# Attention products in two column groups of 64 output rows, run in groups

## The chip, the cores and the metric

The kernel runs on one core of a Trainium2 chip. Its engines work side by side and wait for each other through semaphores: TensorE (PE; PEld is its weight load) multiplies, VectorE (DVE), ScalarE (ACT) and GpSimd (POOL) do the elementwise work, and SyncE (SP) issues most of the transfers. The metric is the device time in microseconds of one execution; a profile of one execution shows what each engine did when.

TensorE multiplies a stationary operand of up to 128 x 128, which is loaded first, by a moving operand. The loaded operand's columns become the rows of the output. In the profile `128*128 128x64` is a product with 128 rows and 128 columns of weights, whose output has 64 elements in each row. A product of plain f32 operands shows as two records, a transpose or a product of the feed-forward's fp32r operands as one.

## What is computed

First a gated linear attention over 4 batches, 8 heads, 768 steps and 48 channels a head; then, on its output `x` (4 x 768 x 384), a Fourier transform over sequence and channels, and a normalized feed-forward layer with 1536 hidden channels:

```python
state = np.zeros((B, H, D, D), dtype=np.float32)
for t in range(S):
    state = alpha[:, :, t, :, None] * state + np.einsum('bhd,bhe->bhde', k[:, :, t], v[:, :, t])
    y[:, :, t] = np.einsum('bhd,bhde->bhe', q[:, :, t], state)
...
u = x + np.real(np.fft.fft(np.fft.fft(x, axis=1), axis=2))
un = (u - mu) / np.sqrt(var + 1e-06)
ch = np.maximum(un @ w_ch1, 0.0) @ w_ch2
return u + ch
```

## The kernel before

The attention takes two heads at a time: a pair lies in 112 partitions, one head in 0 to 47, the other in 64 to 111. The sequence is cut into six chunks of 128 steps. For each of the 16 pairs the function `attn_stages` has eight stages:

- s1 to s3 (DVE mostly): running products of alpha within the chunks, keys divided and queries multiplied by them (`R` and `A`), and the factors `mt` by which the state decays from chunk to chunk.
- s4: five TensorE transposes of the keys to `kt` (128 steps x 112), copied out by ACT.
- s5: the scores of each chunk, one product for each head. Head 0 has its 48 weight rows in partitions 0 to 47, head 1 in 64 to 111, so the two stand in different row groups of the array. ACT copies the scores to `X`, POOL's `affine_select` cuts them to the causal half.
- s6: for each of five chunks one product of keys and values, 112 x 96, both heads at once (line 865). Half of each result mixes the keys of one head with the values of the other; ACT builds masked decay factors `mh` (two operations, line 868), and the DVE multiplication of line 869, which brings the result from PSUM to `tt`, clears that half. Four DVE updates (line 874) then add each chunk's state to the decayed one of the chunk before.
- s7: for each of six chunks, scores times values, one product for each head with 128 output rows and 64 columns (line 888), and, from the second chunk on, queries times state, both heads at once, 96 columns (line 894). Three chunks share a PSUM tile `py`, which ACT copies to the batch's `y` tiles.
- s8: sums and differences for the Fourier transform (DVE).

`mix_stages` then does the transforms with TensorE products and DVE additions, `norm_stages` the normalization with transposes, and `ffn_stages` the feed-forward in 432 products a batch of 384 moving columns each.

Nothing is issued in the order in which it is written. Each call becomes an `Op` in a `Plan`, which simulates all engines with durations of its own (`duration`) and places the instructions one by one (`simulate`): for each engine the operation that is ready first, and among those ready at once the one with the smallest key. The key of batch b's feed-forward is b*1000 + 500 and it is marked `fill`; that of the next batch's attention is b*1000 + 420. So on TensorE attention goes ahead whenever it is ready, and feed-forward fills the rest. The first batch's attention has nothing to fill it and keys below 0; there the planner puts products of a tile of zeros (`zero`, lines 1331 and 1333) into TensorE's long gaps. PSUM is eight banks: three `a`, two `f1`, three `f2`; attention of later batches has the three `a` alone.

Every instruction passes through line 552, so the profile tells them apart by tiles: `a<-vn,w` (also `vn,x`, `wt,x`) is scores times values, `a<-tt,w` queries times state, `a<-vn,kt` keys times values, `a<-w,al` the scores, `a<-cst,al` the transposes of s4, `f<-x,wt` and `f<-wt,h` the feed-forward.

Of the kernel before, what the change touches and what calls it, by code (L numbers as in the profile page):

```python
# [16 lines left out]
AF = mybir.ActivationFunctionType  # L17
ALU = mybir.AluOpType
AX = mybir.AxisListType

B, H, S, D = 4, 8, 768, 48
DM = H * D
DFF = 4 * DM
P = 128
NT = S // P
# [7 lines left out]
CW = 112  # L33
GRP = 64
# [34 lines left out]
LONG = 3.0  # L69
FIRST = 2.8  # L70
NEAR = 3.0
LATE = 4.0
FAR = 12.0
SHORT = 20.0
# [120 lines left out]
class Plan:  # L195
# [120 lines left out]
    def duration(self, op, named, engine):  # L316
        n = op.free
        if "dma" in op.name:
            return 1.05 if engine == "POOL" else 0.05
        if engine == "PE":  # L320
            m = self.region(named["1"])[4]
            if op.name == "transpose":
                return max(m, self.region(named["2"])[4]) / 1200 + 0.002
            if str(named["1"].real(self.base(named["1"])).dtype).endswith("float32"):
                slow = 1.65 if self.stride(named["2"]) > 16 else 1.0
                p0, p1 = self.region(named["1"])[0:2]
                return max(m, slow * n) / (1100 if p1 - p0 <= GRP else 600) + 0.004
            return n / 2240 + 0.003
        if engine == "ACT":
            pointer = 0.094 if any(isinstance(named.get(k), View) for k in ("bias", "scale")) else 0.0  # L330
            slow = 1.8 if self.stride(named["out"]) > 16 and n > 64 else 1.0
            return (0.11 if self.psum(named.get("1")) else 0.14) + slow * n / 1200 + pointer + (0.25 if "accum_out" in named else 0.0)
        if op.name == "memset":
            return n / (960 if engine == "DVE" else 1100) + 0.01
        if engine == "DVE":
            if op.name == "bn_stats":
                return 0.47
            if op.name == "reciprocal":
                return 0.07 + n / 160
            if op.name == "tensor_tensor_scan":  # L340
                return 0.1 + n / 480
            if isinstance(named.get("scalar1"), View):
                return 0.09 + n / 1200
            whole = "bitcast" in [s[0] for s in named.get("out", View(None)).steps]
            pointer = 0.06 if isinstance(named.get("scalar"), View) else 0.0
            return 0.09 + pointer + n / (1920 if whole and op.name == "tensor_scalar" else 960)
        return 0.126 + n / 1094 if op.name == "affine_select" else 0.15 + n / 477
# [44 lines left out]
    def simulate(self, ghost=False, guess=None):  # L392
        ops = self.ops
# [35 lines left out]
        def finish(op, e):  # L429
            t = max(clock[e], start(op, e))  # L430
            return (max(t, held[other[e]]) if op.port and e in held else t) + op.durs[e]
# [4 lines left out]
            due = coming[e][0][0] + shift if coming[e] else 1e9  # L436
            return t + op.durs[e] > due + HOLD[e] and t < due + GRACE

        placed = 0
        while placed < len(ops):  # L440
            placed += 1
            best, spare = None, None
            for e, cand in wait.items():
                if not cand:
                    continue
                now = clock[e]
                times = []
                for n in cand:
                    op = ops[n]
                    t = start(op, e)  # L450
                    if t is None:
                        continue
                    if len(op.engines) > 1:
                        if any(finish(op, o) < finish(op, e) - SLACK[e] for o in op.engines if o != e):
                            continue
                    times.append((t, max(now, t), n))
                if not times:
                    continue
                free = [x for x in times if not blocks(ops[x[2]], e, x[1])] if guess else times
                for some, held_back in ((free, False), (times, True)):  # L460
                    if not some or (held_back and free):
                        continue
                    first = min(x[1] for x in some)
                    key, n, t = min((ops[n].key, n, max(t, now)) for t, late, n in some if late <= first + WINDOW[e])
                    if held_back:
                        if spare is None or t < spare[0]:
                            spare = (t, n, e)
                    elif best is None or t < best[0]:
                        best = (t, n, e)
            best = best or spare  # L470
            assert best is not None, "no instruction can be placed"
            t, n, engine = best
            op = ops[n]
            done[n] = True
            for e in op.engines:
                wait[e].remove(n)
            op.engine, op.dur = engine, op.durs[engine]
            if guess and op.crit:
                for x in coming.values():
                    while x and done[x[0][1]]:  # L480
                        x.pop(0)
                shift = t - guess[n][0]
# [22 lines left out]
            if "dma" in op.name:  # L505
                if op.loose:
                    end = t + (NEAR if op.key < 0 else FAR)
                else:
# [61 lines left out]
def gla_mix_ffn(ctx: ExitStack, tc: tile.TileContext, alpha, chunked, kq, pairkq, v, w1, w2, consts, rowtab, out):  # L570
    nc = tc.nc
    plan = Plan({"PE": nc.tensor, "ACT": nc.scalar, "DVE": nc.vector, "POOL": nc.gpsimd, "SP": nc.sync})
    V, A, G, T, SY = (Engine(plan, e) for e in ("DVE", "ACT", "POOL", "PE", "SP"))
# [45 lines left out]
    def fixed(shape, name, dtype=F32):  # L619
        return plan.fixed(cp.tile(shape, dtype, name=name))  # L620
# [4 lines left out]
    wts = [None] * (NW // 2)  # L625
    loaded = {}
    tts = [fixed([P, NT - 1, 2, D], f"tt{i}") for i in range(2)]
    mhs = [fixed([P, NT - 1, 2], f"mh{i}") for i in range(2)]
    d1 = fixed([P, S], "d1")
    back = fixed([P, S], "back")  # L630
    rec = fixed([P, NC], "rec")
# [2 lines left out]
    ceps = fixed([P, 1], "ceps")  # L634
    zero = fixed([P, 32], "zero")
    ones = fixed([P, 1], "ones")
    hm = fixed([P, 2], "hm")
    rows = fixed([P, 3], "rows", I32)
    bs = fixed([P, 1], "bs")
    fl = fixed([1, 1], "fl", I32)  # L640
# [44 lines left out]

    def setup():
        V.memset(zero, 0.0)
        for hd in range(2):
            V.memset(hm[:, hd : hd + 1], 0.0)
            for r0, n in ((0, 32), (32, 16)):  # L690
                V.memset(hm[GRP * hd + r0 : GRP * hd + r0 + n, hd : hd + 1], 1.0)
        V.memset(d1, 0.0)
        V.memset(back, 0.0)
        V.memset(back[:, C - 1 :: 2 * C], 1.0)
        V.memset(cm63, -63.0)
        V.memset(ceps, 1e-6)
        V.memset(ones, 1.0)
        V.memset(bad, 0.0)
        A.activation(zero[:, 0:1], zero[:, 0:1], AF.Square)
# [44 lines left out]
    def attn_stages(b, hp, i, mixed, last):  # L744
        tt = tts[i]
        pair, tid = b * NP2 + hp, b * NT3 + hp
        first = tid == 0
        e = last if hp == NT3 else {}
# [113 lines left out]
        def s6():  # L862
            pu = psa()
            for a in range(NT - 1):
                T.matmul(pu[0:CW, a * 2 * D : (a + 1) * 2 * D], e["kt"][:, a], loaded["vn", pair][:, 2 * a * D : 2 * (a + 1) * D], start=True, stop=True)
            mh, mt = mhs[i], e["mt"]
            for hd in range(2):
                A.activation(mh[0:CW, :, hd], mt[0:CW, 0 : NT - 1], AF.Copy, scale=hm[0:CW, hd : hd + 1])
            V.tensor_tensor(
                out=tt[0:CW], in0=pu[0:CW, 0 : (NT - 1) * 2 * D].rearrange("p (a h e) -> p a h e", h=2, e=D),  # L870
                in1=mh[0:CW, :, :, None].broadcast_to([CW, NT - 1, 2, D]), op=ALU.mult,
            )
            for a in range(1, NT - 1):
                V.scalar_tensor_tensor(
                    out=tt[0:CW, a], in0=tt[0:CW, a - 1], scalar=mt[0:CW, a : a + 1], in1=tt[0:CW, a], op0=ALU.mult, op1=ALU.add,
                )

        def s7():
            X = e["X"]
            ytiles = mixed()[0]  # L880
            for h2 in range(2):
                py = psa()
                for c in range(3):
                    cc = 3 * h2 + c
                    cs = slice(cc * P, (cc + 1) * P)
                    o = c * 2 * GRP
                    for hd in range(2):
                        T.matmul(
                            py[:, o + hd * GRP : o + (hd + 1) * GRP], X[h2][:, hd, c], loaded["vn", pair][:, (2 * cc + hd) * D : (2 * cc + hd) * D + GRP],
                            start=hd == 0, stop=cc == 0 and hd == 1,  # L890
                        )
                    if cc:
                        yo = py[:, o : o + 2 * GRP].rearrange("p (h e) -> p h e", h=2)[:, :, 0:D]
                        T.matmul(yo, e["A"][0:CW, cs], tt[0:CW, cc - 1], start=False, stop=True)
                yo = py[:, 0 : 6 * GRP].rearrange("p (a h e) -> p a h e", a=3, h=2)[:, :, :, 0:D]
                FL["ev"].copy(ytiles[h2][:, :, hp * 2 * D : (hp + 1) * 2 * D].rearrange("p a (h e) -> p a h e", h=2), yo)

# [389 lines left out]
    for i, f in enumerate(mixing()):  # L1287
# [3 lines left out]
        n = MIX[i] if i < len(MIX) else 0  # L1291
# [214 lines left out]
```

## Time and profile before

| | us |
|---|---|
| median of 3 runs | 504.91 (504.34 to 505.05) |
| the profiled execution | 504.47 |
| its span, first to last instruction | 502.8 |

The profile lists records: start, length, engine, what is written from what, and the shape. Records on PE overlap, since a product's record lasts from its start to the last of its results; the pace of a stream is the distance between starts. A row `start, us, ... xN` of the timeline is N records of one kind in sequence, its length up to the end of the last. A row of the groups gives busy time, mean length in ns, and the idle time of the engine before them with what ended it. A row of the windows gives for each engine the busy time and number of records in a stretch (PE, PEld, DVE, ACT and POOL in this order), then granted clock and transfers.

Where the batches stand in the trace: the first batch's attention runs to 49 us and its transforms to about 70 us; feed-forward of batch 0 starts at 70.2 us and its last product at 189.5, with the second batch's attention (91 to 144 us) and transforms between; that of batch 1 runs from 189.8 to 305.0 with the third's, that of batch 2 from 305.1 to 420.3 with the last one's; feed-forward of batch 3 runs alone from 420.4 us to the end.

### The profile page before, as it was taken

The numbers are of one execution on the slowest core, as the hardware profiler recorded it, in microseconds if no ns is written. First come the engines' busy times: TensorE is split into PE (matmuls) and PEld (weight loads), VectorE is DVE, ScalarE is ACT, GpSimd is POOL, SyncE is SP. The second block draws the span as 40 slices with busy tenths as digits, with TensorE's granted clock in tenths as the row PEclk, the third lists the DMA queues.
The fourth block names the chain that finished last, engine by engine and source line by source line (L and its number), as shares of the span: only waits on it lengthen the run. The fifth ranks groups of instructions, "written<-read, shape, count | busy, mean of one in ns | idle before, by whom it ended". The sixth has DMA issues, their size and how long they took to land.

```text
span 502.8 us, 9312 instructions
## 1 busy us (share of the span) xinstructions
PE 492.5 (98%) x3740; PEld 474.2 (94%) x3740; DVE 312.5 (62%) x685; ACT 187.6 (37%) x413; POOL 65.8 (13%) x83
## 2 busy tenths in 40 slices
PE   7999999999999999999999999999999999999995
PEld 6899989999999999999999999999999999999994
DVE  8877989897779997546799216736585114113112
ACT  4487386537752254532223115323222113111110
POOL 0421222203212001212200001212300000000000
PEclk9999999999999999999999999999999999999998
DMA  8869323337432113521303001200201001001001
GB/s 298 298 192 355 125 64 102 104 73 261 158 104 96 24 56 97 149 107 44 108 1 125 17 0 48 50 25 2 95 0 50 0 1 47 1 1 47 1 0 53
DMA packets 17681, 42.47 MB, mean 84 GB/s; under 512 B 2688, under 2 KB 8000, under 8 KB 17632
## 3 DMA queue, kind: packets, MB, share of 16 engines
q1 hardware_dynamic: 16576, 39.39, 23.5%
q0 software_dynamic: 768, 2.36, 1.7%
q8 instruction: 31, 0.51, 0.4%
q14 instruction: 18, 0.15, 0.1%
q10 hardware_dynamic: 288, 0.07, 0.1%
HBM read 31.97 MB, written 7.08 MB: 78 GB/s over the span
## 4 chain that ended last, share of the span: by engine, by line
PE 95%; ACT 1%; DMA 1%; POOL 1%; SPq 0%; DVE 0%; issue 0%; ACTq 0%
PE f L552 65%; PE a L552 27%; PE f L1333 1%; DMA al<-in_chunked_dram 1%; PE f L1331 1%; PE a L1331 1%; POOL x L552 1%; SPq L552 0%; ACT c L552 0%; DVE y L552 0%; ACT x L552 0%; ACT h L231 0%; ACT L552 0%; ACT f L552 0%; ACT kt L552 0%
## 5 line engine op out<-in xcount | busy, mean ns | idle before, releaser
L552 PE MATMUL f<-wt,h 128*128 128x384 f32 x864 | 178.9, 344 | 0.4 <-ACT h L231 0.4
L552 PE MATMUL f<-x,wt 128*128 128x384 f32 x864 | 176.5, 342 | 0.0
L552 PEld LDWEIGHTS f<-wt,h 128*128 128x128 f32 x864 | 150.3, 188 | 2.3 <-ACT h L231 0.8
L552 PEld LDWEIGHTS f<-x,wt 128*128 128x128 f32 x864 | 150.4, 188 | 1.2 <-issue 0.2
L552 DVE SCALAR_TENSOR_TENSOR h<-f,h 128x384 fp32r<-128x384 f32 x96 | 53.1, 554 | 123.6 <-ACT h L231 122.8
L231 ACT ACTIVATE h<-f 128x384 fp32r<-128x384 f32 x96 | 47.0, 491 | 185.0 <-PE f L552 179.6
L552 POOL TENSOR_SCALAR_AFFINE_SELECT w<-w 128x384 f32<-128x384 f32 x48 | 33.1, 711 | 199.9 <-ACT w L552 199.9
L552 PE MATMUL a<-vn,w 128*128 128x64 f32 x288 | 41.3, 265 | 0.0
L552 PEld LDWEIGHTS a<-vn,w 128*128 128x128 f32 x288 | 39.5, 191 | 0.0
L552 ACT COPY w<-a 128x384 f32<-128x384 f32 (+4 forms) x59 | 26.2, 482 | 26.2 <-PE a L552 26.1
L552 PE MATMUL a<-tt,w 112*128 112x96 f32 x144 | 28.0, 282 | 0.0
L552 DVE TENSOR_TENSOR y<-y,a 128x192 f32<-128x192 f32 (+4 forms) x66 | 20.5, 361 | 8.6 <-PE a L552 8.4
L552 PEld LDWEIGHTS a<-w,al 48*128 48x128 f32 x306 | 19.8, 187 | 5.8 <-ACT w L552 2.2
L552 PE MATMUL a<-w,al 48*128 48x128 f32 x306 | 24.9, 289 | 0.0
L552 ACT COPY y<-a 128x288 f32<-128x288 f32 x29 | 11.6, 399 | 31.9 <-PE a L552 31.8
L552 PEld LDWEIGHTS a<-tt,w 112*128 112x128 f32 x144 | 22.3, 191 | 0.5
L552 DVE TENSOR_TENSOR_SCAN w<-al,d 128x768 f32<-128x768 f32 (+1 forms) x13 | 21.1, 1624 | 2.1 <-PE a L552 1.1
L552 DVE SCALAR_TENSOR_TENSOR y<-f,r,y 128x384 f32<-128x384 f32 x30 | 17.3, 613 | 8.0 <-PE f L552 7.9
L552 DVE SCALAR_TENSOR_TENSOR tt<-tt,w 112x96 f32<-112x96 f32 x64 | 21.2, 331 | 1.3
L552 DVE TENSOR_TENSOR tt<-a,mh 112x480 f32<-112x480 f32 x15 | 9.8, 654 | 19.0 <-PE a L552 19.0
L552 DVE TENSOR_TENSOR_SCAN al<-al,back 128x768 f32<-128x768 f32 (+1 forms) x13 | 21.2, 1633 | 0.2 <-DVE w L552 0.2
L552 POOL DMA_INDIRECT y<-scr,rows x12 | 14.8, 1237 | 48.2 <-DMA scr<-y 45.7
(130 smaller groups left out, 557.3 us busy)
## 6 DMA issues: line engine op xcount, KB each, us to landing
kq<-in_kq_dram SPq DMA_DIRECT2D x10, 768.0 KB, 7.0
wt<-in_w_dram SPq DMA_DIRECT2D x8, 768.0 KB, 7.0
out_dram<-y SPq DMA_DIRECT2D x24, 192.0 KB, 1.9
al<-in_chunked_dram SPq DMA_DIRECT2D x11, 392.0 KB, 3.8
vn<-in_v_dram SPq DMA_DIRECT2D x14, 296.0 KB, 3.1
wt<-in_w_dram SPq DMA_DIRECT2D x8, 384.0 KB, 3.8
scr<-y SPq DMA_DIRECT2D x4, 576.0 KB, 3.7
w<-w SPq DMA_DIRECT2D x28, 48.3 KB, 2.1
```

What stands on the lines that cost most here:

```text
L231: return lambda out, x: e.activation(out, x, AF.Relu)
L552: op.ins = op.fns[op.engine](*[real(a) for a in op.args], **{k: real(x) for k, x in op.kwargs.items()})
L1331: short = lambda *b: nc.tensor.matmul(bank(*b)[0:32, 480:512], zero.real(), zero.real(), start=True, stop=True)
L1333: long = lambda *b: nc.tensor.matmul(bank(*b)[0:32, 384:512], zero.real(), wide.real(), start=True, stop=True)
```

## The change

In s7 each product of scores and values, and each of queries and state, becomes two, with half of the weight columns: output rows 0 to 63 and 64 to 127. In s6 the product of both heads becomes one for each head, 48 x 48, into output rows 0 to 47 and 64 to 111 of the same columns; only what belongs together is computed. The DVE multiplication becomes one for each head, straight with `mt`; the masked factors `mhs`, the mask `hm` and its memsets go, and `tts` are set to zero once at the start, since the mixed halves are no longer written. The four updates stay.

The planner counts such products at 1100 columns a microsecond instead of 600, and holds attention back on TensorE: after a feed-forward product, if feed-forward could go on, the ready operations that aren't `fill` and have a key of at least 400 are left out of the choice as long as their durations sum to less than 1.3 us and the first of them has been ready for less than 1 us.

```diff
+TOGETHER = 400.0
+ENOUGH = 1.3
+PATIENCE = 1.0
...
-                return max(m, slow * n) / (1100 if p1 - p0 <= GRP else 600) + 0.004
+                return max(m, slow * n) / (1100 if p1 - p0 <= GRP or m in (D, GRP) else 600) + 0.004
...
-        placed = 0
+        placed, filled = 0, False
...
+                if e == "PE" and filled:
+                    due = [x for x in times if x[0] <= now and not ops[x[2]].fill and ops[x[2]].key >= TOGETHER]
+                    if due and any(x[0] <= now and ops[x[2]].fill for x in times):
+                        if sum(ops[x[2]].durs[e] for x in due) < ENOUGH and now - min(x[0] for x in due) < PATIENCE:
+                            times = [x for x in times if x not in due]
...
+            if engine == "PE":
+                filled = op.fill
...
-        for hd in range(2):
-            V.memset(hm[:, hd : hd + 1], 0.0)
-            for r0, n in ((0, 32), (32, 16)):
-                V.memset(hm[GRP * hd + r0 : GRP * hd + r0 + n, hd : hd + 1], 1.0)
+        for tt in tts:
+            V.memset(tt, 0.0)
...
-                T.matmul(pu[0:CW, a * 2 * D : (a + 1) * 2 * D], e["kt"][:, a], loaded["vn", pair][:, 2 * a * D : 2 * (a + 1) * D], start=True, stop=True)
-            mh, mt = mhs[i], e["mt"]
-            for hd in range(2):
-                A.activation(mh[0:CW, :, hd], mt[0:CW, 0 : NT - 1], AF.Copy, scale=hm[0:CW, hd : hd + 1])
-            V.tensor_tensor(
-                out=tt[0:CW], in0=pu[0:CW, 0 : (NT - 1) * 2 * D].rearrange("p (a h e) -> p a h e", h=2, e=D),
-                in1=mh[0:CW, :, :, None].broadcast_to([CW, NT - 1, 2, D]), op=ALU.mult,
-            )
+                for hd, r0 in enumerate((0, GRP)):
+                    T.matmul(
+                        pu[r0 : r0 + D, a * D : (a + 1) * D], e["kt"][:, a, r0 : r0 + D],
+                        loaded["vn", pair][:, (2 * a + hd) * D : (2 * a + hd + 1) * D], start=True, stop=True,
+                    )
+            mt = e["mt"]
+            for hd, r0 in enumerate((0, GRP)):
+                r = slice(r0, r0 + D)
+                V.tensor_tensor(
+                    out=tt[r, :, hd], in0=pu[r, 0 : (NT - 1) * D].rearrange("p (a e) -> p a e", e=D),
+                    in1=mt[r, 0 : NT - 1, None].broadcast_to([D, NT - 1, D]), op=ALU.mult,
+                )
...
-                        T.matmul(
-                            py[:, o + hd * GRP : o + (hd + 1) * GRP], X[h2][:, hd, c], loaded["vn", pair][:, (2 * cc + hd) * D : (2 * cc + hd) * D + GRP],
-                            start=hd == 0, stop=cc == 0 and hd == 1,
-                        )
+                        for lo in (0, GRP):
+                            T.matmul(
+                                py[lo : lo + GRP, o + hd * GRP : o + (hd + 1) * GRP], X[h2][:, hd, c, lo : lo + GRP],
+                                loaded["vn", pair][:, (2 * cc + hd) * D : (2 * cc + hd) * D + GRP], start=hd == 0, stop=cc == 0 and hd == 1,
+                            )
                     if cc:
-                        yo = py[:, o : o + 2 * GRP].rearrange("p (h e) -> p h e", h=2)[:, :, 0:D]
-                        T.matmul(yo, e["A"][0:CW, cs], tt[0:CW, cc - 1], start=False, stop=True)
+                        for lo in (0, GRP):
+                            yo = py[lo : lo + GRP, o : o + 2 * GRP].rearrange("p (h e) -> p h e", h=2)[:, :, 0:D]
+                            T.matmul(yo, e["A"][0:CW, cs.start + lo : cs.start + lo + GRP], tt[0:CW, cc - 1], start=False, stop=True)
```

More of the change, by code (lines that the diff above doesn't have):

```diff
@@ L627, in gla_mix_ffn @@
     tts = [fixed([P, NT - 1, 2, D], f"tt{i}") for i in range(2)]
-    mhs = [fixed([P, NT - 1, 2], f"mh{i}") for i in range(2)]
     d1 = fixed([P, S], "d1")
@@ L636, in gla_mix_ffn @@
     ones = fixed([P, 1], "ones")
-    hm = fixed([P, 2], "hm")
     rows = fixed([P, 3], "rows", I32)
```

## The prediction

> **What bounds the kernel now.** I read the page's busy shares first, then the chain that ended last, then PE's waits.
>
> ```profile
> span 502.8 us, 9312 instructions
> PE 492.5 (98%) x3740; PEld 474.2 (94%) x3740; DVE 312.5 (62%) x685; ACT 187.6 (37%) x413; POOL 65.8 (13%) x83
> ...
> PE 95%; ACT 1%; DMA 1%; POOL 1%; SPq 0%; DVE 0%; issue 0%; ACTq 0%
> ...
> PE a L1331 <- ACT zero L552: 3.3, 1, 3.3
> PE a L552 <- POOL x L552: 0.5, 2, 0.3
> ```
>
> TensorE is busy 98% of the span, is 95% of the chain, and its longest waits (us in total, times, longest) come to 3.8 us. Up to about 70 us part of that business is filler on a tile of zeros (L1331, L1333). From 73.5 us on the feed-forward products of one batch fill every hole that the attention of the next leaves, so there a microsecond taken from PE's stream is a microsecond off the end, as long as what follows is ready. What the change touches is named by group; from 73.5 to 420 us:
>
> ```profile
> L552 PE MATMUL a<-vn,w 128*128 128x64 f32 x288 | 41.3, 265 | 0.0
> ...
> L552 PE MATMUL a<-tt,w 112*128 112x96 f32 x120 | 23.0, 280 | 0.0
> L552 PE MATMUL a<-vn,kt 128*112 128x96 f32 x120 | 14.4, 266 | 0.0
> ```
>
> One f32 product leaves two records, so these are 12 head pairs with 12 value products, 5 state products and 5 outer products (keys by values) each. Busy time and mean overlap, so cost is read from the distance between starts, in the timeline:
>
> ```profile
> 41.62 1.06 PEld L552 LDWEIGHTS a<-wt,h 128*112 128x112 f32 x10
> 42.60 1.42 PEld L552 LDWEIGHTS f<-wt,x 128*128 128x128 f32 x12
> ...
> 16.92 1.28 PEld L1331 LDWEIGHTS a<-zero 128*32 128x32 f32 x38
> 18.24 0.19 PEld L552 LDWEIGHTS a<-vn,x 128*128 128x128 f32 x1
> ...
> 48.70 7.30 PE L1333 MATMUL f<-zero 128*32 128x128 f32 x64
> ```
>
> Ten loads of 112 columns take 0.98 us to the next row, 0.098 each; twelve of 128 columns (1.42 - 0.19)/11 = 0.112. These products move only 64 or 96 rows, and still come at the pace of the load: they are bound by weight columns. Loads of 32 columns came at 0.032 (1.32 us to the next row for 38, less about 0.1 of switching). Where 128 rows move against 32 columns, 7.30/64 = 0.113 each: then the moving side binds. So a record takes about 0.058 for 64 columns or rows, 0.045 for 48 and 0.085 for 96, all estimates between these rows.
>
> **The change, part by part.** Before, in that stretch: 288 x 0.112 + 120 x 0.112 + 120 x 0.098 = 57.5 us.
>
> *Column groups.* Each product becomes two, of half the columns, into the lower and upper 64 output rows. If two such records run side by side, a pair takes 0.058 (values), 0.085 (state, 96 moving rows), 0.045 (outer products, 48 columns and rows): 288 x 0.058 + 120 x 0.085 + 120 x 0.045 = 32.3 us, 25.2 less. If they take turns, twice that, 64.6 us, 7.1 more. These are the two ends. No row of before has two column groups at work; the nearest is the pair of row groups in the scores:
>
> ```profile
> 201.82 0.33 PE L552 MATMUL f<-wt,h 128*128 128x384 f32 x1
> 202.09 0.94 PE L552 MATMUL a<-w,al 48*128 48x128 f32 x12
> 202.96 0.45 PE L552 MATMUL f<-wt,h 128*128 128x384 f32 x1
> 203.24 0.34 PE L552 MATMUL f<-wt,h 128*128 128x384 f32 x1
> 203.41 0.34 PE L552 MATMUL f<-x,wt 128*128 128x384 f32 x1
> ```
>
> Twelve records of 128 columns start within 0.94 - 0.29 = 0.65 us (0.29 is one record's mean length in its group), 0.108 for two: both loads and both streams ran side by side. Column groups differ in one thing, that both read the same 128 partitions. But a feed-forward product moves 384 four-byte rows in about 0.175 us (203.24 to 203.41), 2200 a microsecond, and an f32 record 128 in 0.113, half as many. So reading for two f32 streams is within what the read path does already. I take side by side.
>
> *Switching.* From the start at 201.82 to that at 203.41 lie 1.59 us; three feed-forward products (those at 201.82, 202.96 and 203.24, 0.52) and six pairs at 0.108 (0.65) leave 0.42. So one run of tiled records between feed-forward ones costs about 0.42 beside its work: the stream empties, and the first loads on both sides are not hidden. A run over the full array costs nothing of the kind:
>
> ```profile
> 206.34 0.33 PE L552 MATMUL a<-vn,w 128*128 128x64 f32 x2
> 206.48 0.95 PE L552 MATMUL f<-x,wt 128*128 128x384 f32 x4
> 207.27 0.51 PE L552 MATMUL f<-wt,h 128*128 128x384 f32 x2
> ```
>
> Two records (0.224) and four feed-forward products (0.70) take 0.93. With column groups the value, state and outer products become tiled runs; with 64 columns the first load is 0.05 shorter, so 0.37 a run. In the timeline after 73.5 us there are 26 runs of scores and 60 of the three groups that change, 45 of these straight after feed-forward; the first and last:
>
> ```profile
> 93.26 0.54 PE L552 MATMUL a<-vn,kt 128*112 128x96 f32 x4
> 93.73 0.94 PE L552 MATMUL a<-w,al 48*128 48x128 f32 x12
> ...
> 350.31 0.41 PE L552 MATMUL a<-tt,w 112*128 112x96 f32 x2
> ```
>
> *Grouping* exists for this: after a feed-forward product, ready attention products wait until they come to 1.3 us or the oldest is 1 us old. By the planner's durations a pair then has 0.5 (transposes) + 1.45 (scores) + 0.5 + 1.5 + 0.9 = 4.9 us, so 3.7 groups if all were full; dribbles end some sooner, so I take 4, 48 for 12 pairs, of which 46 hold a tiled product. Some 22 runs of scores pay the 0.42 already, so 24 more pay 0.37, 8.9 us, and ten changes inside a group between full and tiled 0.15, 1.5 us: 10.4 together. Unmerged, 45 x 0.37 + 15 x 0.15 = 18.9. The added wait holds back only attention on PE; behind it feed-forward goes on. The copies of ACT, the selects of POOL and the updates of DVE that wait for those products start up to 1 us later at each step, which costs nothing while there is feed-forward work left to run.
>
> *No masks.* 32 ACT operations go and one DVE multiplication per pair becomes two:
>
> ```profile
> L552 ACT ACTIVATE mh<-w,hm 112x5 f32<-112x5 f32 x32 | 8.4, 301 | 3.7 <-DVE w L552 3.6
> ...
> L552 DVE TENSOR_TENSOR tt<-a,mh 112x480 f32<-112x480 f32 x15 | 9.8, 654 | 19.0 <-PE a L552 19.0
> L552 DVE TENSOR_TENSOR z<-f 128x288 f32<-128x288 f32 x16 | 6.8, 449 | 0.0
> L552 DVE TENSOR_TENSOR z<-w 128x96 f32<-128x96 f32 x16 | 3.7, 250 | 0.0
> ```
>
> Two of 240 elements lie between the last two rows, about 0.40 each, so DVE gains 0.15 a pair, 2.4 us in all, and ACT loses 9.6. Both lie beside PE's stream: worth nothing there; without that cover at most 2.4 us. The mask's memsets at the start give way to two of 480 elements, before the first data lands. No DMA is added or moved.
>
> *The first batch.* Here PE binds only in places:
>
> ```profile
> 37.29 0.84 PE L552 MATMUL a<-w,al 48*128 48x128 f32 x12
> ...
> 42.69 1.48 PE L552 MATMUL f<-wt,x 128*128 128x64 f32 x12
> 44.09 1.01 PE L1331 MATMUL f<-zero 128*32 128x32 f32 x26
> ```
>
> From 38 to 44 us it runs value and state products without filler; halved they would end 2 to 3 us sooner, less two or three switches; then comes DVE's chain. I take 1.5, between 0 and 3.
>
> **The sum.** 25.2 - 10.4 + 1.5 = 16.3 less. The profiled run took 504.47 (span 502.8 and 1.67 around it); the median shown is 504.91. 504.47 - 16.3 = 488.2; I say 488.5. With 36 tiled groups and 3 us in the first batch, 483; with 55 and nothing in the first batch, 493.
>
> The Trainium skill, "TensorE: Matmul & The Clock Gate", "Measured speedup vs the span model", has three column tiles at 2.38 times one. By an estimate from that page two records take 1.26 times as long, 40.7 us for 32.3, and the sum would be 497.
>
> **The rivals.**
>
> *Together, but the gain shrinks* (493 to 503). Either runs stay unmerged: 25.2 - 18.9 + 1.5 = 7.8, 497. Or the second batch gives its share back, since DVE is its near bound:
>
> ```profile
> 74.00:190.00 116.00, 116.00 (x811) 111.42 (x812) 101.91 (x197) 60.43 (x128) 18.70 (x20) 1.00 0.34 109
> ```
>
> DVE is busy 101.91 of 116 us there (the fourth figure); if its front kept its pace, feed-forward would run out first and a third of 14.8, 4.9 us, would be lost: 493. Against it: four pairs' share leaves DVE 14 us of slack for 5.
>
> *The groups take turns, slower.* One mechanism: both column groups' weights and rows pass the same 128 partitions one after the other. Then 64.6 - 57.5 + 10.4 = 17.5 more, 522; if only the loads take turns (0.116, 0.116, 0.09), 58.1 + 10.4 - 57.5 = 11 more, 515.5. It decides as soon as a pair takes more than (57.5 - 10.4)/32.3 = 1.46 times one record. For it: no row shows it otherwise, and every f32 record here is bound by loading. Against it: the scores' pairs and the feed-forward rate.
>
> *Loads wait for streams.* If a load couldn't overlap a product that has the same rows, a pair would take 0.116, state 0.143, outer 0.09: 61.4 + 10.4 - 57.5 = 14.3 more, 519. Against it stand the 32-column records: load and stream of one column group, every 0.032, which is one of the two and not their sum. The Trainium skill states this rule in "TensorE: Matmul & The Clock Gate", Part 3, "The mechanism" (a load overlaps running products only in another row group); by that row the trace disagrees.
>
> *It does nothing*, gain and switches cancelling within 1 us: 504.5.
>
> **How the numbers follow.** Forecast 483 to 493: 0.54. Together with a smaller gain: 0.22. No change (within 0.2%, 1.0 us, about what a measurement of this kernel can tell): 0.04. Turns 0.15 and waiting loads 0.05, both slower: 0.20. Faster is 0.54 + 0.22 = 0.76. The range: 482 to 509 leaves out some 0.04 below and 0.16 above. Predicted 488.5.
>
> **What would show it.** Right: value records of 64 columns start in twos, two within 0.06 us, state records two within 0.085; fewer than 50 tiled runs after 73.5 us; feed-forward of the second batch ends some 5 us sooner than 189 us; no wait of PE over 1 us. Wrong: starts at 0.058 each, one by one (turns); 60 or more tiled runs (no merging); PE waiting for DVE before 190 us (second batch).

## The result and the profile after

| | before | after |
|---|---|---|
| median, us | 504.62 (504.23 to 505.05, 4 runs) | 493.25 (493.09 to 493.32, 4 runs) |
| profiled execution, us | 504.47 | 493.09 |
| its span, us | 502.8 | 491.4 |

The ratio is 0.9775, 95% interval 0.9761 to 0.9789: 11.4 us less, where 16.3 were forecast. It lies in the range of 482 to 509, just above the likeliest case's own 483 to 493 and so, by a hair, in that of the rival "together, but the gain shrinks".

The page after, its first two lines, and the waits of PE (us in total, times, longest):

```profile
span 491.4 us, 10884 instructions
...
PE 481.6 (98%) x4532; PEld 449.1 (91%) x4532; DVE 312.3 (64%) x693; ACT 182.9 (37%) x382; POOL 59.7 (12%) x86
```

```profile
PE a L1343 <- ACT zero L562: 3.3, 1, 3.3
PE f L562 <- ACT x L562: 0.4, 1, 0.4
PE f L562 <- DVE x L562: 0.3, 1, 0.3
```

TensorE still binds: 98% of the span, 792 records more in 10.9 us less busy time. The two short waits come back in the last experiment. The groups that changed, from 73.5 to 415 us:

```profile
L562 PE MATMUL a<-vn,w 128*64 128x64 f32 x576 | 27.4, 224 | 0.0
...
L562 PE MATMUL a<-tt,w 112*64 112x96 f32 x240 | 21.8, 258 | 0.0
...
L562 PE MATMUL a<-vn,kt 128*48 128x48 f32 x240 | 7.9, 212 | 0.0
```

Twice the records of before; values and outer products are busy for 27.4 and 7.9 us where they had 41.3 and 14.4. The state products fall little, 23.0 to 21.8, since busy time counts a record to its end, which hides the pace. The pace and the price of a run stand in the timeline:

```profile
94.67 0.51 PE L562 MATMUL f<-x,wt 128*128 128x384 f32 x2
95.11 0.69 PE L562 MATMUL a<-vn,w 128*64 128x64 f32 x16
95.72 0.44 PE L562 MATMUL f<-x,wt 128*128 128x384 f32 x1
...
96.18 0.51 PE L562 MATMUL f<-x,wt 128*128 128x384 f32 x2
...
225.34 0.50 PE L562 MATMUL a<-tt,w 112*64 112x96 f32 x8
225.67 0.40 PE L562 MATMUL a<-vn,w 128*64 128x64 f32 x8
```

The 16 value records start in twos, the two of a pair within 0.01 us. Their 0.69 us less the last one's 0.22 are seven steps from pair to pair, the first of 0.11 and the others of 0.058, as forecast for side by side. Eight state records take 0.33 to the next row, 0.083 for two (0.085 forecast): 96 moving rows bind there. Outer products come at 0.045 for two. From 94.67 to 96.18 lie 1.51 us: four feed-forward products (two at 94.67, one at 95.72, and one between it and 96.18) at 0.175, eight pairs at 0.058, and 0.35 that no work fills. That is what this run costs beside its products; 0.37 was forecast.

Where the time came from, by the first feed-forward product of each batch in the timelines:

| feed-forward of batch starts at, us | 0 | 1 | 2 | 3 | span |
|---|---|---|---|---|---|
| before | 70.2 | 189.8 | 305.1 | 420.4 | 502.8 |
| after | 70.5 | 185.5 | 297.5 | 408.8 | 491.4 |

The three stages between get shorter by 4.6, 3.3 and 4.0 us, 11.9 together; the first batch gives nothing (0.3 the other way), and the end, which has no attention, nothing either.

### The profile page after: what moved, and what is told of

It is laid out like the page before. It is cut to its first block, busy times and chain, and to the rows that moved or that the text cites. A ratio compares the mean times of both kernels' runs of the same rounds, so it can differ in the third digit from the quotient of the medians.

```text
span 491.4 us, 10884 instructions
## 1 busy us (share of the span) xinstructions
PE 481.6 (98%) x4532; PEld 449.1 (91%) x4532; DVE 312.3 (64%) x693; ACT 182.9 (37%) x382; POOL 59.7 (12%) x86
## 4 chain that ended last, share of the span: by engine, by line
PE 97%; DVE 2%; ACT 0%; ACTq 0%; issue 0%
PE f L562 67%; PE a L562 24%; PE a L1343 3%; PE f L1345 2%; PE f L1343 2%; DVE y L562 1%; DVE al L562 0%; ACT L562 0%; DVE st L562 0%; ACTq L562 0%; DVE x L562 0%; DVE mv L562 0%; ACT zero L562 0%; DVE w L562 0%; DVE back L562 0%
## 5 line engine op out<-in xcount | busy, mean ns | idle before, releaser
L562 PE MATMUL f<-wt,h 128*128 128x384 f32 x864 | 174.4, 341 | 0.0
L562 DVE SCALAR_TENSOR_TENSOR h<-f,h 128x384 fp32r<-128x384 f32 x96 | 53.2, 555 | 115.6 <-ACT h L234 115.0
L562 POOL TENSOR_SCALAR_AFFINE_SELECT w<-w 128x384 f32<-128x384 f32 x48 | 25.2, 547 | 204.4 <-ACT w L562 204.4
L562 PE MATMUL a<-vn,w 128*64 128x64 f32 x576 | 27.4, 224 | 0.0
L562 DVE TENSOR_TENSOR tt<-a,w 48x240 f32<-48x240 f32 x30 | 12.1, 405 | 23.2 <-PE a L562 22.9
L562 PEld LDWEIGHTS a<-vn,w 128*64 128x64 f32 x576 | 23.6, 137 | 3.2 <-issue 3.0
L562 PE MATMUL a<-tt,w 112*64 112x96 f32 x288 | 26.3, 259 | 0.0
L562 DVE TENSOR_TENSOR y<-y,a 128x192 f32<-128x192 f32 (+6 forms) x66 | 20.6, 361 | 1.7 <-PE a L562 1.6
L562 PEld LDWEIGHTS a<-tt,w 112*64 112x64 f32 x288 | 14.8, 136 | 6.0 <-issue 2.3
L562 DVE TENSOR_TENSOR z<-f 128x288 f32<-128x288 f32 (+3 forms) x40 | 19.7, 532 | 0.0
```

The source lines that it names most:

```text
L562: op.ins = op.fns[op.engine](*[real(a) for a in op.args], **{k: real(x) for k, x in op.kwargs.items()})
```

## The experiments

My theory: two column groups run side by side when their products are neighbours in the stream, which halves the work; tiled runs among feed-forward, and changes between whole and tiled products, take a good part of it back; gathering limits their number. Rivals: narrower weights are cheaper by themselves; gathering is the gain; the first batch or the second is bound elsewhere. A tiled group below is a stretch without feed-forward that holds a tiled product (scores included), counted in the timeline after 70 us: 24 before, 53 after. Inside them stand 14 changes between whole and tiled products before, 26 after. Times are medians and ratios are to the kernel before, which took 504.26 to 504.70 beside them.

The distance from the feed-forward product before a tiled group to the second one after it, less all products from the one to the other at their paces (0.175 for feed-forward; 0.058, 0.085 and 0.045 for pairs of values, state and outer products; 0.112 for a pair of scores or a whole record), is what the group costs: 22.8 us for the 53, 0.43 each with the changes inside. Before, 20 of the 24 can be read so, at 0.44 each.

**The order of the column groups.** All products of the lower 64 rows of a PSUM tile, then all of the upper:

```diff
-                    for hd in range(2):
-                        for lo in (0, GRP):
+                for lo in (0, GRP):
+                    for c in range(3):
...
+                        for hd in range(2):
```

and in s6 the heads outside, the chunks inside.

> The change with the same products in another order: within a PSUM tile all products of output rows 0 to 63 first, then all of rows 64 to 127, so that neighbours in the stream use the same column group. Theory (the gain comes from two column groups running side by side when their products are neighbours): value records start 0.058 us apart one by one, state records 0.085, outer products 0.045, which adds 288 x 0.058 + 120 x 0.085 + 120 x 0.045 = 32 us after 73.5 us: 520 to 530 us. Rival (narrower weights alone make the products cheaper, or the array takes them side by side in any order): 493 to 497 us.

Measured 534.14 (ratio 1.0577, 1.0554 to 1.0600). Its timeline, a run of value records:

```profile
110.57 0.68 PE L562 MATMUL a<-vn,w 128*64 128x64 f32 x8
```

Eight records take what sixteen take above. The starts of feed-forward are 77.2, 208.0, 329.6 and 449.5 us: the stages between grow by 34.0 us over the change's, 2.7 of it more waits of PE; 32 were forecast. The first batch grows by 6.7, more than the 5 or so that the upper end of 530 left for it, hence 534. So neither the smaller weights nor the array's own choice makes the gain: neighbours in different column groups do.

**Without gathering.** `TOGETHER = 1e9`.

> The change with its column groups but without the rule that gathers attention on TensorE (the threshold of keys set out of reach). Theory (each tiled run among feed-forward costs about 0.37 us, and gathering saves runs): some 60 to 70 tiled runs after 73.5 us instead of 50, time 496 to 499 us against 493.25 with the rule. Rival (the gathering is worth nothing, the gain is all from the column groups): 493 us within 0.7. Second rival (the rule costs more by delaying the second batch than it saves): 491 us or less.

Measured 501.34 (ratio 0.9937, 0.9920 to 0.9954): 8.1 more than with the rule, more than I expected. There are 73 runs of the three groups (60 to 70 expected) and 82 tiled groups instead of 53, and the stages take 346.8 us instead of 338.3. Column groups alone thus give 3.4 of the 350.2 us of before; 29 tiled groups fewer give 8.5 on top, 9.2 without the waits of PE in the change, 0.3 each. The later two stages alone say the same: 6.3 us for 19 groups.

**Gathering alone**, in the kernel before.

```diff
+                if e == "PE" and filled:
+                    due = [x for x in times if x[0] <= now and not ops[x[2]].fill and ops[x[2]].key >= TOGETHER]
...
```

> The kernel before with the gathering rule alone, its products whole and its masks kept. Theory (gathering pays only because tiled runs are dear; here just the scores are tiled): runs of scores straight after feed-forward stay near 20 of 22, so 503.5 to 505.5 us against 504.6. Rival (gathering is itself a good part of the gain): 501 us or less.

Measured 503.41 (ratio 0.9979, 0.9969 to 0.9988): some 0.2% faster, just below what was expected. The groups among feed-forward fall from 108 to 67, the tiled ones stay at 24, and the stages take 1.6 us less. All of that lies in the second batch's stage (117.4 us instead of 119.6); the later two take 231.2 instead of 230.6, though 21 groups fewer stand there. So it is not shown that fewer whole groups are worth anything; the rival that gathering makes the gain falls.

**State updates over the whole array with masks**, as before (s6, `mhs` and `hm` put back).

> The change with the state updates as before: one product of keys and values for both heads over the full array, masks and the one masked multiplication; values and state stay in column groups. Theory (outer products cost 11.8 us before and 5.4 in two column groups after 73.5 us, and most follow a tiled run of scores anyway): 5 to 7 us slower than the change, 498 to 500 us. Rival (this part gives nothing, since it only adds tiled runs): 492.5 to 494 us.

Measured 501.14 (ratio 0.9936, 0.9920 to 0.9953), 7.9 slower than the change. The stages take 344.0 us, 5.7 more, as expected; feed-forward starts at 72.5 us, 2.0 later, which I had not. But 4.0 of the 5.7 lie in the second batch's stage. In the later two it is 1.7, though whole outer products cost 80 x (0.098 - 0.045) = 4.2 us more there: there are 27 tiled groups instead of 34, which gives most of the rest back, against 25 changes inside them instead of 15. So the rival is half right: splitting the outer products does add tiled runs. How much of the 5.7 us is the part's own worth stays open, since the order of the plan alone can move the second batch's stage by some 5 us (the first batch, below).

**Queries times state whole**, the rest as in the change:

```diff
-                        for lo in (0, GRP):
-                            yo = py[lo : lo + GRP, o : o + 2 * GRP].rearrange("p (h e) -> p h e", h=2)[:, :, 0:D]
-                            T.matmul(yo, e["A"][0:CW, cs.start + lo : cs.start + lo + GRP], tt[0:CW, cc - 1], start=False, stop=True)
+                        yo = py[:, o : o + 2 * GRP].rearrange("p (h e) -> p h e", h=2)[:, :, 0:D]
+                        T.matmul(yo, e["A"][0:CW, cs], tt[0:CW, cc - 1], start=False, stop=True)
```

> The change with queries times state as one whole product again, values and outer products in column groups; so the stream changes between whole and tiled products inside a group, some 64 times more often after 73.5 us. Theory (such a change costs some 0.13 us inside a group, as the array empties and a load is not hidden): 64 x 0.13 = 8 us and 120 x 0.027 = 3.2 us for the wider records, in all 503 to 509 us with the first batch. Rival (only runs between feed-forward products cost anything, since those change the operands' type too): 3.2 us and little else, 496 to 498 us.

Measured 510.57 (ratio 1.0120, 1.0103 to 1.0138), slower than before the change. Its timeline:

```profile
325.78 0.45 PE L562 MATMUL a<-vn,w 128*64 128x64 f32 x8
326.16 0.46 PE L562 MATMUL a<-tt,w 112*128 112x96 f32 x2
326.55 0.45 PE L562 MATMUL a<-vn,w 128*64 128x64 f32 x8
```

From the first to the third start lie 0.77 us: four pairs (0.23), two whole records (0.22) and 0.31 for two changes, 0.155 each. There are 91 changes inside groups instead of 26. It is not the feed-forward's other type that costs, since both sides are f32 here. The stages of the third and fourth batch's attention, where PE waits for nothing, take 232.0 us instead of 223.3: less 80 x 0.027 for the wider records, 6.5 us for 50 changes more, 0.13 each, as expected. The rest of the loss is in the first batch (2.1 us) and in the second's stage, 120.6 us instead of 115.0 with 2.7 of waits in it. In all it is 1.6 us above what was expected.

**The first batch.** Values and state whole in it alone.

> The change, but with whole products of values and state in the first batch alone. Theory (the first batch's end is set by VectorE's work, which takes up what PE gains there): the first feed-forward product still starts at 70.5 us within 0.6, though PE ends the first batch's attention some 2 us later than the 46.6 us of the change. Rival (the first batch gains from column groups and something else costs it as much): 72 to 73 us. The time of the whole may move by a few us more, since the planner then orders the second batch otherwise.

The first feed-forward product starts at 70.5 us again. ACT's last copy to the `y` tiles starts at 47.76 us, 46.62 in the change and 48.81 before: whole products cost 1.1 us there (some 2 expected). So with the change PE is 2.2 us earlier than before at that point, and nothing comes of it. DVE's busy time (fourth figure) in the stretch up to the transforms, before and after:

```profile
42.30:55.90 13.60, 13.60 (x146) 12.89 (x144) 13.13 (x34) 5.04 (x10) 2.05 (x2) 1.00 0.75 288
```

```profile
39.00:56.20 17.20, 17.20 (x252) 15.83 (x247) 16.84 (x41) 10.01 (x18) 3.43 (x4) 1.00 0.78 297
```

DVE works through 97 and 98% of both stretches: sums for the transform, state updates, and the splitting of weights, in an order that the planner shuffles. It takes up what PE gains. Where PE's products end later than before (50.2 us instead of 48.7, with the state whole, 510.57 above), DVE waits for ACT's last copy of them to `y`, and the first feed-forward product starts at 72.6 us.

```profile
50.74 0.46 DVE L562 TENSOR_TENSOR w<-y,y 128x288 f32<-128x288 f32 x1 [0.82 <-ACT y L562]
```

Before, the same wait was 0.33 us; in the change there is none. The order of the plan moves this start too: with the masked updates it is 72.5 us, though PE's products end at 47.6. So that DVE is the bound here fits the runs, but none of them holds the order still. The whole run with the first batch's products whole took 499.27: with another order, the second batch's stage became 119.9 us long, with 2.9 of PE's waits in it, though its products are those of the change (115.0). So a difference of some 5 us in that stage alone can come from the order of the plan, and the later two stages tell more.

**How long to gather.** `PATIENCE = 2.2` for all batches, the limit of work as in the change:

> The change with 2.2 us of age for all batches. Theory (the second batch's front is bound by VectorE and its own chain, so holding its attention back runs feed-forward dry): feed-forward of the second batch starts 3 to 6 us later than the 185.5 us of the change, with waits of PE before it, while the later two stages get 2 to 3 us shorter together; 494 to 498 us. Rival (the second batch follows PE alone, so fewer tiled runs help there too): 489 to 491 us, feed-forward of the second batch no later than in the change.

Measured 494.78 (ratio 0.9819, 0.9802 to 0.9837). Two of PE's waits, at 186.1 and 182.4 us:

```profile
PE a L562 <- DVE mv L562: 1.8, 1, 1.8
PE a L562 <- DVE y L562: 1.4, 1, 1.4
```

The second batch's feed-forward starts at 187.7 us, 2.2 later than in the change (3 to 6 expected), though there are 12 tiled groups fewer in all; the last product of batch 0's feed-forward starts at 180.7 us, and PE runs dry after it. The later two stages get 3.0 shorter. So in the second batch VectorE's chain is close behind, and holding attention back makes it the bound. Two versions with longer limits for keys from 1000 on alone:

```diff
+                        later = min(ops[x[2]].key for x in due) >= 1000.0
+                        enough, patience = (ENOUGH_LATER, PATIENCE_LATER) if later else (ENOUGH, PATIENCE)
-                        if sum(ops[x[2]].durs[e] for x in due) < ENOUGH and now - min(x[0] for x in due) < PATIENCE:
+                        if sum(ops[x[2]].durs[e] for x in due) < enough and now - min(x[0] for x in due) < patience:
```

> The change with other limits for keys from 1000 on (third and fourth batch's attention): gather to 2.6 us or 1.5 us of age; below that 1.3 and 1.0 as in the change. Theory (each tiled group among feed-forward costs a third of a microsecond, a change inside a group some 0.13; the later batches have 30 us of feed-forward in reserve and the second has none): five or six tiled groups and some nine inner changes fewer, so 2 to 4 us less than the change, 489.5 to 491.5 us. Rival (waiting longer delays the later batches' chains and gives it back): 493 us or more.

Measured 490.39 (ratio 0.9715, 0.9702 to 0.9728), as expected: six tiled groups fewer, and from the second to the last batch's feed-forward 219.7 us instead of 223.3.

> As the run before it, but 3.0 us of age for keys from 1000 on. Theory: four tiled groups fewer still, so 1 to 1.5 us below the run before it unless a later batch's front then ends after the feed-forward before it, 488.5 to 491 us. Rival (reserve used up): PE waits before the feed-forward of the third or last batch, 493 us or more.

Measured 491.07 (ratio 0.9735, 0.9721 to 0.9748): no better, though there are four tiled groups fewer still, as expected. The transposes that feed the next batch's feed-forward now stand right at the end of the one before (294.2 and 403.3 us, 0.9 us ahead of the next start), so the reserve is used up. PE waits 0.3 us there, and from the last batch's first feed-forward product to the end are 84.5 us instead of 82.6 in the change:

```profile
292.63 1.73 PE L566 MATMUL f<-wt,h 128*128 128x384 f32 x9
294.19 0.71 PE L566 MATMUL a<-cst,f 128*128 128x128 f32 x5
295.05 1.69 PE L566 MATMUL f<-x,wt 128*128 128x384 f32 x8
```

**Shorter first, longer later**: 0.4 us of age in the second batch; 2.6 us of work or 1.8 us of age afterwards.

> Gathering with 0.4 us of age for keys below 1000 (second batch) and 2.6 us of work or 1.8 us of age above. Theory (held back less, the second batch's chain ends sooner, and the 1 us that PE waits before its feed-forward at 184 to 187 us in the change goes, at the price of some four tiled groups more there; the later batches gain as in the run with 1.5 us): feed-forward of the second batch starts at 184 to 186 us with less than 0.5 us of waits before it, 488.5 to 490.5 us. Rival (that wait is not the rule's doing): waits as in the change and the time 490.5 to 492 us.

Measured 489.33 (ratio 0.9696, 0.9681 to 0.9711), the fastest here, 3.9 below the change. Where feed-forward passes from the first batch to the second, in the change and then in this version:

```profile
183.52 1.11 PE L562 MATMUL f<-wt,h 128*128 128x384 f32 x5
184.62 0.55 PE L562 MATMUL a<-cst,f 128*128 128x128 f32 x3
185.53 1.48 PE L562 MATMUL f<-x,wt 128*128 128x384 f32 x7 [0.36 <-ACT x L562]
187.32 0.96 PE L562 MATMUL f<-x,wt 128*128 128x384 f32 x4 [0.31 <-DVE x L562]
```

```profile
182.33 2.96 PE L566 MATMUL f<-wt,h 128*128 128x384 f32 x16
185.13 0.38 PE L566 MATMUL a<-cst,h 128*128 128x128 f32 x2
185.26 0.59 PE L566 MATMUL f<-wt,h 128*128 128x384 f32 x2
185.70 0.69 PE L566 MATMUL f<-x,wt 128*128 128x384 f32 x3
```

The two waits (0.67 us) are gone, so they were the rule's doing. But the stage is as long as in the change (115.2 and 115.0 us): five more tiled groups took their place. The later two stages get 5.1 us shorter, and 1.6 come back after the last batch's first feed-forward product (84.2 us to the end instead of 82.6).

## Why the prediction was right, and where it was off

The mechanism was right, and every term that was off made the gain smaller. What came is the upper end that the prediction gave its own case, 493 us "with 55 and nothing in the first batch": 53 tiled groups and nothing in the first batch. The mark of fewer than 50 tiled runs was missed; that no wait of PE would be over 1 us came true (the longest after the start of the kernel is 0.36), and batch 0's feed-forward, which is what ends at 189.5 us before, ends 5 us sooner.

- *PE bounds the kernel from 73 us on*: right. Stage by stage the time follows PE's stream, up to 0.67 us of waits.
- *Column groups run side by side*: right, and shown. A pair takes 0.058, and the same products in another order 34 us more in the stages. The two rivals that make it slower fall with it: taking turns happens only between neighbours of the same column group, and loads don't wait for streams (two loads and two streams of 64 in 0.058 us).
- *The factor of 1.26* worked out from the Trainium skill, "TensorE: Matmul & The Clock Gate", "Measured speedup vs the span model": by that estimate the sum was 497. The pairs here show no such loss (0.058 for two, and for one by itself in the other order).
- *Switching, 10.4 us*: the term that was off most. The price was right: 10.4 for 24 more groups is 0.43 each, changes inside included, and 0.43 was measured. The count was too low: 53 tiled groups stand there, not 46, 29 more than before, and 29 x 0.43 = 12.5. The changes inside were near (12 more, ten forecast). "Four groups a pair" was too few: age alone ends many of them, since 2.2 us of it instead of 1.0 leave 41.
- *No merging, 18.9 us*: near. Without gathering 25.2 - 3.4 = 21.8 us were paid.
- *Grouping costs nothing while feed-forward lasts*: right for the later batches, wrong for the second, by 0.67 us in the change and more with longer limits. The rival that DVE bounds that stage was right in kind and far smaller than the 4.9 us that it was given.
- *The first batch, 1.5 us*: wrong, nothing. PE gained 2.2 us there, and DVE was busy 97 to 98% of the time.
- *No masks*: two DVE products take 0.405 us each, as forecast (12.1 us for 30), and DVE's busy time is as before. That splitting these products adds tiled groups, so that in the later two stages only 1.7 us come of it, was not foreseen.

Added up: 25.2 - 12.5 - 0.7 (waits) = 12.0 for the 11.9 us that the stages show; 0.5 are lost at the start and the end, which leaves the 11.4 of the span. That it meets within 0.1 is in part luck: each term is good to some tenths of a microsecond only.

## What to carry to other kernels

Two products of 48 or 64 output rows each ran side by side here in two column groups, at the pace of one, where they were neighbours in the stream; look for weight loads that set the pace. Count the changes of form before splitting: here 25 us of gain came with 12 to 13 of switching, and one sort of product left whole between tiled ones turned the gain into a loss. Gather tiled work where the filler has reserve, and not where the held-back chain is the next bound.

## What the runs showed of the hardware

- Two column groups share all 128 input partitions, and two f32 records still took 0.058 us (95.11 us in the change), as long as one of 64 columns by itself (110.57 us in the other order).
- A change between whole and tiled f32 products cost 0.155 us in the place shown and 0.13 on the mean of 50. A tiled run between feed-forward products cost 0.35 in the place shown, and a tiled group 0.43 on the mean of 53; of the 0.35, 0.11 falls on the feed-forward product after it (95.72 to 96.18 us, 0.46 for two that otherwise take 0.35).
- The order within one PSUM tile alone was worth 41 us (534.14 and 493.25) with the same set of products.
